# Polysketch attention and a multiplicative FFN on one core: six w3 blocks brought into w_out's column order by GpSimd's addition instead of by VectorE's transpose

## The chip, the cores and the metric

One Trainium2 chip, one of its cores. The metric is device time in microseconds of one execution of the whole program, as a median of several runs. Inputs of the reference that are float64 (S1, S2 and the four FFN matrices) lie in memory as 64-bit words, and the kernel turns them into float32 itself.

## The reference

```python
# batch 4, heads 4, seq 1088, head_dim 32, r = 8
def phi(x):
    a = np.einsum('rd,bhsd->bhsr', S1, x)
    b = np.einsum('rd,bhsd->bhsr', S2, x)
    return np.einsum('bhsi,bhsj->bhsij', a, b).reshape(*x.shape[:-1], r * r)
q_p, k_p = (phi(q), phi(k))
kv = np.einsum('bhsf,bhsd->bhfd', k_p, v)
z = np.sum(k_p, axis=2)
num = np.einsum('bhsf,bhfd->bhsd', q_p, kv)
den = np.einsum('bhsf,bhf->bhs', q_p, z)[..., None] + 1e-06
attn = (num / den).astype(np.float32)
# bridge: (B,H,S,D) -> (B*S, H*D); n_tokens 4352, d_model 128, d_ff 1024
a = x @ w1
b = x @ w2
h = a * b @ w3            # w3 is 1024 x 1024
out = (h @ w_out).astype(np.float32)
```

## The kernel before

The kernel is a list of named steps. Each step issues one or a few instructions on one engine, and the text ORDER at the head of the file says in which order all of them are issued. Each engine (TensorE for matmuls and transposes into PSUM, VectorE, ScalarE, GpSimd, and SyncE, which issues most DMAs) works through its own steps in that order, and waits at a step whose inputs or whose buffer are not ready. A second text, POOL, names the steps of a choosable kind that run on GpSimd; those not named there (or in ACTS) run on VectorE. A third, SLOTS, says which buffer each new tile takes: "x" (three buffers for k, v and q), "raw" (three, for raw weights), "l", "m", "s" and the eight PSUM banks "b". Nothing is scheduled at run time.

Names of the steps that matter below (b or g is a batch or group number):

- k{b}.load, .loadr, .max, .g, .lead, .rest, .gram0 to .gram4, .Gm, .Gt, .Ga, .Gb, .T, .N, .kT, .ab, .abt, .kp0, .kp1, .kv, .kq: the side of k. k is cut into a leading part and a rest (lead on ScalarE or VectorE, rest a subtraction), gram products give denominators' statistics, kp is the product of the two sketches, kv the product with v. kr0 and kr1 are the last 64 positions of two batches each; kr0.tr transposes them on TensorE.
- q{g}.tr, .max, .l2, .l1, .rm, .C0, .A0, .C1 (sketch products on TensorE), .Ct, .At (VectorE transposes), .sm, .st, .sh, .sl, .sc, .al, .p01, .p2, .p12, .dn, .de, .rc, .bs, .phi0 and .phi1 (the feature product), .pT0 and .pT1 (VectorE transpose), .x0 (TensorE, gives the attention output), .xT: the side of q. q0 and q1 have 512 positions, q2 and q3 too, q4 and q6 1024, qr the remainders.
- w{n}.load, .c, .m (ScalarE: upper words to float32 but for three bits of exponent, lower words scaled to an integer), .j (VectorE: a shift left by three), .a0 and .a1 (GpSimd: the integer addition of the lower part, in two halves of 512 columns): conversion of the weights. w0 and w1 hold halves of w1 and w2, w2 is w_out, w3 to w10 are the eight blocks of 128 rows of w3.
- f{ko}.t, .m, .o: the fold. The product of w3 and w_out is formed once (w3o = w3 @ w_out, eight blocks), since the FFN has nothing between the two. f.t transposes a w3 block (blocks 0 and 1 by TensorE in t0 and t1 with copies c0 and c1; blocks 2 to 7 by VectorE), f.m multiplies by w_out, f.o copies to SBUF. Both ways take the columns c, c+8, c+16, ... of w3, since w_out is loaded with 8 neighbouring rows in each partition.
- g{g}.{c}a, .c, .b, .m, .o: the FFN for group g (512 positions; gr has 256) and column block c: a and b are the matmuls with w1 and w2, c is ScalarE's copy of a, m is VectorE's product, o the matmul with w3o. g.oT and g.st bring the output out.
- warm*: matmuls on zeros that fill TensorE at the start.

The FFN's a and b matmuls of early groups are spread between the attention steps of later batches, so TensorE has work while VectorE prepares q and k.

Of the kernel before, what the change touches and what calls it, by code (L numbers as in the profile page):

```python
# [14 lines left out]
I32 = mybir.dt.int32  # L15
# [3 lines left out]
ALU = mybir.AluOpType  # L19
# [10 lines left out]
        "012345670123462764153276410574210437201420126754201640321407215350712047201326014235071352"  # L30
        "401547613720641602374651534672013635012731504705021746501456732142531602563623654321034562"
        "017567034617460315614370165425601351036450126305412036531024135605242556245645340467416701"
        "45701530507113274",
    "k_g": "0101",
    "l": "0123456789abc01243598a67b291a45c73b1a859076b2c9436071acb4326097a540cb261348",
    "m": 
        "0123456789abcdefghijklmnopqrstuv031425786badrenfoht514m3cjl6hqgsn58dmchr4qdj16u9krf2pi8b13"
        "ef750av9obrtlehnp4jfisbmugk07redgl5qrvocp6fre5ahldm2obl4thgq1pnreaq8g1npt7rglj925lujev62s4"
        "i9ajnrb1pe",
    "q_m": "0101101",  # L40
    "raw": "012012101201201",
    "s": "012345671302456703265140376215073",
    "x": "012010210210",
# [4 lines left out]
BY_PE = (0, 1)  # L48
# [4 lines left out]
    k0.Nf k0.Nh k0.Nl k0.kp0 k1.kp0 k2.kp1 k3.kp1 q0.p12 q0.p2 q0.phi0 q1.al q1.p12 q1.p2 q2.al q2.p12  # L53
    q2.phi0 q3.al q3.p2 q3.phi0 q4.al q6.al q6.p12 q6.p2 q6.phi0 qr.p12 qr.phi0 s.Pp s.blk s.blkh s.rest
    s.sum
# [18 lines left out]
v1.loadr q0.xT warm12 kr1.ab warm11 g0.2a g0.1a k2.load q1.pt0 q1.pt1 w1.j k1.Ga g0.3a g0.2c k1.kT1 q1.pc0 w1.a1
q1.pc1 k1.Gb k1.ab k1.T0 k1.T1 q1.x q3.tr g0.1c warm15 w0.a1 q1.restT q3.max g0.1b q2.tr k1.abt q1.xT k2.max g1.6b
g0.2b q2.max w1.a0 q2.l2 g1.3a s.AR k2.g k1.Ta k1.Tb g0.2m k2.lead0 k1.Ts q3.l2 g0.3c g1.3c q2.l1 k2.rest0 g0.7a g1.5a
g1.2a w2.load g1.5c w3.c k1.N0 q3.l1 g1.2c k1.N1 s.RC k1.kp1 q2.load g0.7c k1.Na g0.1m q4.tr k2.gram0 k2.gram1
k2.gram2 k2.gram3 k2.gram4 warm13 g1.0a kr1.abc g1.0c w3.m g1.6a g1.6c w4.load k2.Gm q4.max k1.Nb g0.0a g0.5a g0.5c
q2.rm g0.4b g1.2b q3.rm g0.0c k1.Nr w4.c k2.Gt g1.6m g0.7b q2.C0 k2.Ga w3.j g1.2m k2.Gb k3.zero w4.j k1.kp0 w4.m w3.a1
q2.A0 k3.loadr w4.a0 g0.7m q2.C1 q2.Ct q2.At q2.sm q2.st q2.sh q2.sl q2.sc q2.p01 k0.kqt w4.a1 g0.4a g0.6a g1.7a f1.t0  # L80
g0.6b g0.0b k0.kq w2.c g0.6c q4.l2 f1.c0 w3.a0 w2.j g0.0m g0.4c w2.m g1.5b g0.4m g1.1a g1.4a g1.1c g1.7c f0.t1 q2.al
v1.load w5.load f0.t0 w5.m k1.kv0 q2.p2 w2.a0 f0.c0 q2.p12 g0.6m k1.kv2 k1.kv3 q2.dn g1.5m k1.kv1 k2.T0 k2.T1 k1.kvr
k2.Ta q2.de q2.restT w9.load k1.kvc f0.c1 q2.rc k2.Tb k2.Ts q2.bs q3.C0 q3.A0 q3.C1 k1.kqt w2.a1 k1.kq w9.c f1.t1
q3.load g1.3b f0.m q3.Ct q3.At g1.7b k2.N0 q3.sm q2.phi0 f1.c1 f0.o q2.pT0 k2.N1 q2.x0 g1.4c q3.st g1.3m q3.sh w9.m
w5.c warm26 k2.Na q3.sl w8.load q3.sc f1.m g1.0b q2.xT0 k2.Nb w5.j k2.Nr v2.zero g1.7m q3.p01 q3.al g2.0a q4.l1 f1.o
g2.4b g2.0b q4.rm w9.j w5.a0 w6.load q4.C0 w9.a0 g2.0c w8.c q4.A0 w8.m q4.C1 w8.j g2.0m g2.4a g2.4c g1.0m q4.Ct q4.At
q3.restT w5.a1 g1.4b g2.2a g0.5b g2.3a g2.1a k3.load f2.t g2.2c w6.c w6.m g2.1c f2.m w9.a1 f6.t g1.1b f6.m k3.max w6.j
k3.g g0.5m q4.sm q3.p2 w8.a1 g2.3c kh2.load w7.load k2.kT0 g2.4m g2.1b g2.6a w6.a1 w6.a0 w8.a0 g2.5a g1.1m k3.lead0
g2.5c q3.p12 f5.t k3.rest0 g2.5b g2.3b f5.m g2.6c f5.o g2.7a f2.o w7.m f3.t q3.dn q3.de q3.rc f3.m q3.bs g2.6b q3.phi0
g2.1m g2.3m g2.5m g1.4m g2.2b q3.pT0 g2.7c f3.o w7.c k2.kT1 q3.x0 k3.gram0 k3.gram1 kr1.kp g2.2m q3.xT0 f6.o g2.6m  # L90
w7.j w7.a1 k3.gram2 k3.gram3 k2.ab k2.abt k3.gram4 k3.Gm g3.1a g3.5a g1.0o g3.6a g1.1o g1.6o g3.3a k3.Gt v3.zero
k2.kp1 qr.max k3.Ga v3.loadr w10.load g3.3c w7.a0 q4.st f4.t g3.1c g0.3b q4.sh q4.sl g3.6c qr.l2 w10.c g0.3m k2.kp0
q4.sc q4.p01 w10.j g3.5c k3.Gb w10.m g3.2b w10.a0 w10.a1 g3.4a g3.7a g2.7b qr.l1 v2.loadr v2.load kh3.load g3.4c g3.7c
q6.tr q6.max q6.l2 g0.0o g0.1o f4.m f4.o q6.l1 g0.2o g2.7m g0.6o g0.3o g0.5o g3.7b k2.kv0 q4.al k3.T0 q4.p2 q4.p12
q4.dn q4.de k3.T1 k2.kv3 f7.t q4.rc k3.kT0 k2.kv1 k2.kv2 k2.kvr warm28 g1.3o k2.kvc f7.m g3.2a q4.bs q4.phi0 f7.o
g3.2c q4.phi1 qr.rm k3.Ta v3.load g3.0a q4.pT0 k3.Tb g3.2m g0.4o g1.4o g0.7o k2.kqt k2.kq g1.5o g1.2o g3.0c g0.oT
q4.pT1 k3.Ts g3.7m k3.kT1 q4.x0 q4.x1 q4.xT1 q4.xT0 k3.N0 k3.N1 g1.7o k3.ab k3.Na k3.Nr k3.Nb q6.rm q6.C0 q6.A0 q6.C1
k3.abt g1.oT q6.Ct g2.0o g5.7a g3.3b g2.4o g4.0a g4.0c g5.7c q6.At q6.sm k3.kp0 k3.kp1 g2.6o g2.5o g4.1a g3.0b g3.0m
g3.3m k3.kv0 k3.kv1 q6.st k3.kv3 k3.kv2 k3.kvr qr.C0 qr.A0 k3.kvc qr.C1 k3.kqt g1.st g0.st qr.Ct qr.At g4.3a g2.3o
g5.0a q6.sh q6.sl q6.sc q6.p01 q6.al q6.p2 q6.p12 g5.4a qr.sm k3.kq g4.1c g4.4a g5.1b g5.1a g5.4c g5.1c g5.0c g4.7a  # L100
q6.dn qr.st g5.1m q6.de g4.3c qr.sh q6.rc g3.4b g2.2o g5.6a q6.bs g4.4c q6.phi0 g5.6c q6.phi1 g3.4m q6.pT0 g2.1o g2.7o
g4.0b q6.pT1 g5.0b g3.0o g4.7c g4.0m q6.x0 g2.oT q6.x1 g5.7b g5.2b q6.xT1 q6.xT0 qr.sl qr.sc g5.0m qr.al qr.p01 qr.p2
g3.6b g4.3b g3.6m qr.p12 g6.6a g6.0a g6.6b g6.0c g6.6c g5.2a g3.1b g6.6m g4.3m g6.4a g5.3a g5.5a g5.7m g5.2c g6.4c
g3.1m qr.dn qr.de g5.2m g7.1a g4.5a qr.rc qr.bs qr.phi0 g5.5c g5.3c g5.4b g5.4m g4.5c g3.5b g4.5b g7.1c g3.4o g6.4b
g7.7a g3.5m g6.1a g5.3b g2.st g4.5m g7.6a g6.1c g7.7c g4.4b g6.5a g5.5b g7.0a g6.4m qr.pT0 g5.3m g7.0c g3.3o g4.4m
g5.5m qr.x0 g3.1o g3.6o g3.2o g6.5c g7.6c qr.xT0 g3.5o g4.6a g4.7b g6.3a g5.0o g4.6c g7.5b g7.6b g7.6m g4.7m g6.1b
g6.2b g5.1o g6.5b g6.7a g6.3c g6.7c g6.5m g7.0b g5.2o g5.4o g5.6b gr.0a gr.0c g6.1m g5.6m g5.3o g7.0m g7.5a g5.5o
g6.2a g7.5c g7.0o g7.4a g6.2c g7.4c gr.6a gr.6c g3.7o g7.3a g7.4b g5.6o g6.0b g7.5m g7.4m g6.2m gr.4b gr.0b gr.0m
g7.3b g4.2a g7.3c g3.oT g4.2c gr.1a g5.7o g5.oT gr.1c gr.6b g4.1b gr.6m g7.3m g6.7b g6.7m g4.0o g4.1m g7.6o g4.4o
g4.1o g6.0m g7.2a g7.2c gr.4a gr.4c g7.1b g6.0o g7.5o g7.7b g7.1m g7.7m gr.4m g6.3b g6.5o g7.2b g7.2m gr.3b gr.3a  # L110
# [11 lines left out]
def make_steps(ctx, tc, q, k, v, S1, S2, moe_w1, moe_w2, moe_w3, moe_w_out, out):  # L122
# [3 lines left out]
    r = S1.shape[0]  # L126
    DM, DF = moe_w1.shape
    assert (B, H, S, D, r, DM, DF) == (4, 4, 1088, 32, 8, 128, 1024)
    NC = DF // 128
# [18 lines left out]
    def on(name):  # L148
        return pool if name in POOL else act if name in ACTS else dve
# [236 lines left out]
    def conv(n):  # L386
# [41 lines left out]
        @step(f"w{n}.j")  # L428
        def _():
            on(f"w{n}.j").tensor_scalar(made(), x["c"].bitcast(I32), 3, None, ALU.logical_shift_left)  # L430
# [1125 lines left out]
```

## Time and profile before

| | us |
|---|---|
| median of 3 runs | 255.98 (255.94 to 256.82) |
| profiled execution | 256.87 |
| its span, first to last instruction | 255.0 |
| TensorE matmuls busy | 247.4 |
| VectorE busy | 170.3 |
| ScalarE busy | 99.6 |
| GpSimd busy | 63.4 |

The granted clock of TensorE is 1.00 throughout. Of the rows of a group, the first figures after the bar are the busy time in us and the mean time of one instruction in ns, then the idle time just before them and what ended it. In a timeline a row has its start, its length in us, the engine, the source line, the operation, out<-in, the shape, and in brackets the idle time before it and its releaser.

### The profile page before, as it was taken

To read this page: it belongs to the slowest core of one execution; us is meant where nothing else is said; L and a number is where in the kernel's file an instruction comes from. 1 tells how busy PE (TensorE), PEld (TensorE's weight loads), DVE (VectorE), ACT (ScalarE), POOL (GpSimd) and SP (SyncE) were. 2 spreads that over 40 slices of the span, in tenths; PEclk is the share of its full clock that TensorE was granted. 3 is DMA by queue.
4 is the path that set the end of the run, shared out by engine and by line. 5 is a ranking of instruction groups with operands and counts; after the bars stand their busy time and mean duration, and the time that the engine had idled before them with its cause. 6 is when DMAs were issued, how large, how long until landed. Compare 5 with 4: busy or idle time off the path is not lost.

```text
span 255.0 us, 6027 instructions
## 1 busy us (share of the span) xinstructions
PE 247.4 (97%) x2519; PEld 139.8 (55%) x2519; DVE 170.3 (67%) x357; ACT 99.6 (39%) x185; POOL 63.4 (25%) x99
## 2 busy tenths in 40 slices
PE   8799999999999998999999999999999999999994
PEld 6689746456835575465544544444444445445454
DVE  3799999999999998998887667455202314432222
ACT  3668558886866541274131141241320132101000
POOL 2385560475364534422003044010000000000000
PEclk9999999999999999999999999999999999999999
DMA  6959383692897200990005000200000002200133
GB/s 181 282 160 269 125 322 141 177 234 69 226 219 200 48 3 3 195 228 2 3 3 82 5 0 1 41 1 3 0 0 0 3 0 36 46 0 0 29 54 63
DMA packets 30267, 22.02 MB, mean 86 GB/s; under 512 B 21152, under 2 KB 25504, under 8 KB 29856
## 3 DMA queue, kind: packets, MB, share of 16 engines
q1 hardware_dynamic: 29552, 21.05, 32.2%
q10 hardware_dynamic: 688, 0.59, 0.7%
q8 instruction: 20, 0.33, 0.5%
q14 instruction: 7, 0.06, 0.1%
HBM read 19.40 MB, written 2.23 MB: 85 GB/s over the span
## 4 chain that ended last, share of the span: by engine, by line
PE 74%; DVE 19%; DMA 2%; issue 2%; SPq 1%; POOL 1%; ACT 0%; DVEq 0%; POOLq 0%
PE ps_o L1462 22%; PE a_ps L1439 20%; PE b_ps L1449 19%; DVE ab L1455 3%; DVE w3T L463 2%; PE ps_g L595 2%; PE ps_x L1399 2%; DMA kr<-in_k_dram 2%; PE ps_or L1469 1%; PE ps_w3o L469 1%; PE ps_kv L705 1%; PE ps_ac L1285 1%; DVE kk L587 1%; DVE k_m L180 1%; DVE pT L1388 1%
## 5 line engine op out<-in xcount | busy, mean ns | idle before, releaser
L1455 DVE TENSOR_TENSOR ab<-ffa,b_ps 128x512 f32<-128x512 f32 (+1 forms) x72 | 45.3, 650 | 53.7 <-PE b_ps L1449 45.5
L1444 ACT COPY ffa<-a_ps 128x512 f32<-128x512 f32 (+1 forms) x72 | 38.4, 564 | 103.3 <-PE a_ps L1439 97.7
L1439 PE MATMUL a_ps<-xT,w 128*128 128x512 f32 (+1 forms) x144 | 66.0, 572 | 0.0
L1449 PE MATMUL b_ps<-xT,w 128*128 128x512 f32 (+1 forms) x144 | 65.9, 570 | 0.0
L1462 PE MATMUL ps_o<-ab,w3o 128*128 128x512 f32 x128 | 61.3, 595 | 0.0
L1439 PEld LDWEIGHTS a_ps<-xT,w 128*128 128x128 f32 x144 | 26.6, 191 | 29.1 <-issue 23.4
L1449 PEld LDWEIGHTS b_ps<-xT,w 128*128 128x128 f32 x144 | 26.6, 191 | 27.5 <-issue 23.4
L1462 PEld LDWEIGHTS ps_o<-ab,w3o 128*128 128x128 f32 x128 | 23.8, 191 | 24.7 <-issue 24.3
L436 POOL TENSOR_TENSOR w3c<-w3c,cv_m 128x512 int32<-128x512 int32 x16 | 20.6, 1306 | 22.4 <-DVE w3c L430 10.1
L469 PEld LDWEIGHTS ps_w3o<-wo,w3T 128*128 128x128 f32 x128 | 15.3, 192 | 4.5 <-issue 2.1
L469 PE MATMUL ps_w3o<-wo,w3T 128*128 128x128 f32 x128 | 15.7, 276 | 0.5 <-DVE w3T L463 0.5
L221 PE MATMUL idle_ps<-zeros 128*128 128x256 bf16 x72 | 13.4, 317 | 1.0 <-DVE zeros L193 1.0
L1478 DVE STREAM_TRANSPOSE oT<-ps_o 128x512 f32<-128x512 f32 x8 | 5.7, 708 | 12.0 <-PE ps_o L1462 12.0
L229 ACT ACTIVATE cv_c<-raw 128x1024 f32<-128x1024 f32 x11 | 12.9, 1172 | 1.3 <-DMA raw<-in_moe_w_dram 1.3
L1380 POOL TENSOR_TENSOR ph<-s_al,s_bs 128x1024 f32<-128x1024 f32 (+1 forms) x4 | 8.0, 1991 | 20.2 <-DVE s_bs L1370 20.2
L417 ACT ACTIVATE cv_m<-raw 128x1024 int32<-128x1024 uint32 x11 | 13.0, 1189 | 0.0
L463 DVE STREAM_TRANSPOSE w3T<-w3c 128x1024 f32<-128x1024 f32 x6 | 12.1, 2034 | 0.0
L613 POOL TENSOR_TENSOR kp<-kabt 128x1024 f32<-128x1024 f32 x3 | 5.8, 1946 | 18.5 <-DVE kabt L681 18.2
L221 PEld LDWEIGHTS <-zeros 128*128 128x128 bf16 x72 | 7.7, 114 | 4.0 <-issue 1.2
L1388 DVE STREAM_TRANSPOSE pT<-ph 128x1024 f32<-128x1024 f32 (+1 forms) x7 | 8.0, 1151 | 1.7 <-POOL ph L1380 1.7
L1410 ACT COPY xT<-ps_x 128x128 f32<-128x128 f32 (+2 forms) x20 | 4.6, 326 | 10.0 <-PE ps_x L1399 7.0
L180 DVE TENSOR_REDUCE k_m<-k 128x1 f32<-128x1152 f32 (+1 forms) x5 | 5.4, 1086 | 3.1 <-DMA k<-in_k_dram 3.1
(243 smaller groups left out, 296.6 us busy)
## 6 DMA issues: line engine op xcount, KB each, us to landing
raw<-in_moe_w_dram SPq DMA_DIRECT2D x24, 256.0 KB, 5.9
qh<-in_q_dram SPq DMA_DIRECT2D x4, 544.0 KB, 4.2
out_dram<-oT SPq DMA_DIRECT2D x33, 64.0 KB, 2.0
raw<-in_moe_w_dram SPq DMA_DIRECT2D x4, 512.0 KB, 6.0
raw<-in_moe_w_dram SPq DMA_DIRECT2D x2, 1024.0 KB, 8.1
k<-in_k_dram SPq DMA_DIRECT2D x3, 512.0 KB, 5.2
v<-in_v_dram SPq DMA_DIRECT2D x2, 512.0 KB, 4.0
raw<-in_moe_w_out_dram SPq DMA_DIRECT2D x1, 1024.0 KB, 5.8
```

The costliest lines, as they stand in the source:

```text
L221: pe.matmul(t, zeros, bview(zeros, [[0, 2], [1, 128]]), start=True, stop=True)
L229: act.activation(dst, hi.bitcast(F32), ACT.Prelu, scale=2.0 ** -112, alpha=-2.0 ** 32)
L417: act.mul(x["m"], words(0).bitcast(U32), 2.0 ** -29)
L436: pool.tensor_tensor(d, d, x["m"][:, i * 512:(i + 1) * 512], ALU.add)
L463: dve.transpose(w3T[ko].rearrange("p s (i r) -> p s i r", r=32), bview(w3c[ko], [[1, NC], [256, 4], [NC, 32]]))
L469: pe.matmul(t["o"], w3T[ko][:, c], wo[:, c], start=c == 0, stop=c == NC - 1)
L1388: dve.transpose(s["pT"][:, cut], s["ph"][:, cut])
L1439: pe.matmul(x["a"][:, :w], w_of(0, c), xT[g][:, c0:c0 + w], start=True, stop=True)
L1444: act.copy(x["s"][:, :w], x["a"][:, :w])
L1449: pe.matmul(x["b"][:, :w], w_of(1, c), xT[g][:, c0:c0 + w], start=True, stop=True)
L1455: dve.tensor_mul(ab_sb[g, c][:, c0:c0 + w], x["s"][:, :w], x["b"][:, :w])
L1462: pe.matmul(o_ps[g], w3o[:, c], ab_sb[g, c], start=c == 0, stop=c == NC - 1)
```

## The change

In w5 to w10 (w3's blocks 2 to 7) the shift w.j now works in place in cv_c, and GpSimd's addition writes its sum to a new w3c tile in another order of columns: column 8a + b of each 256 goes to place 32b + a. Its two inputs are read in order, and each next word is written 32 words (128 bytes) further, in runs of eight. The VectorE transpose f.t then reads 32 neighbouring columns where it read every eighth. Blocks 0 and 1, and the other weights, are converted as before and as whole blocks; blocks 0 and 1 are still transposed by TensorE.

```diff
         @step(f"w{n}.j")
         def _():
-            on(f"w{n}.j").tensor_scalar(made(), x["c"].bitcast(I32), 3, None, ALU.logical_shift_left)
+            d = x["c"].bitcast(I32) if 3 <= n and n - 3 not in BY_PE else made()
+            on(f"w{n}.j").tensor_scalar(d, x["c"].bitcast(I32), 3, None, ALU.logical_shift_left)
 
         for i in range(2):
             @step(f"w{n}.a{i}")
             def _(i=i):
+                if 3 <= n and n - 3 not in BY_PE:
+                    if i == 0:
+                        made()
+                    d, c, m = (y[:, i * 512:(i + 1) * 512].rearrange(f"p (j {o}) -> p j a b", j=2, **z) for y, o, z in (
+                        (x["d"].bitcast(I32), "b a", {"a": 32}), (x["c"].bitcast(I32), "a b", {"a": 32}),
+                        (x["m"], "a b", {"a": 32})))
+                    pool.tensor_tensor(d, c, m, ALU.add)
+                    return
                 d = x["d"].bitcast(I32)[:, i * 512:(i + 1) * 512]
                 pool.tensor_tensor(d, d, x["m"][:, i * 512:(i + 1) * 512], ALU.add)
...
-                dve.transpose(w3T[ko].rearrange("p s (i r) -> p s i r", r=32), bview(w3c[ko], [[1, NC], [256, 4], [NC, 32]]))
+                dve.transpose(w3T[ko].rearrange("p s (i r) -> p s i r", r=32), bview(w3c[ko], [[32, NC], [256, 4], [1, 32]]))
```

With it POOL, SLOTS and ORDER are new as a whole. On GpSimd and no longer on VectorE are k1.kp1, k2.rest0, k3.kp0, q0.phi1, q2.p2, q3.p12, q4.phi1, qr.p2 and s.low; the other way went q0.phi0, q2.al, q3.phi0, q6.p12, q6.p2, qr.p12, s.blkh and s.rest. The number of instructions on each engine is the same.

In ORDER, at the front, kr0.tr leaves its place ahead of k0.gram0 and comes behind k0.N1:

```diff
-k0.max1 k0.g k0.tr1 k0.lead0 warm5 c.act k0.tr0 s.words k0.lead1 s.pair k0.rest0 k0.rest1 s.low kr0.load kr0.tr
-k0.gram0 k0.gram1 k0.gram2 s.lead k0.gram3 s.sum s.rest k0.gram4 s.T s.four s.tc s.P s.R k0.kT0 q0.tr warm1 k0.Gm
...
+warm18 s.four s.lead warm8 warm12 k0.rest1 s.low s.sum k0.gram0 k0.gram1 k0.gram2 k0.gram3 q0.tr k0.gram4 s.rest s.T
...
+s.Pp k1.max q0.C0 k0.N0 k0.N1 k0.abc0 warm25 k0.kp0 v0.loadr kr0.tr q0.sma k0.kT1 k0.Na k0.ab1 q0.sta q1.l2 w0.m k0.Nb
```

In SLOTS, "x" gives k1 the buffer of k0 (it had one of its own, and v0 had k0's):

```diff
-    "x": "012010210210",
+    "x": "012020120201",
```

SyncE's loads at the front are now k0.loadr, s, q0, w0, k1, k1.loadr, kr0, v0.loadr, v0, w1 (before: k0.loadr, s, q0, kr0, k1, k1.loadr, w0, v0, q1, v0.loadr), and v3.load comes behind g1.st.

On VectorE the steps between q2's and q3's transposes are now: q2.pT0, k2.Ts, q3.st, q3.sh, q3.sl, q3.sc, k2.Na, g1.0m, g0.3m, k2.Nb, w8.j, q3.p01, k2.Nr, q4.rm, g1.3m, w5.j, g2.2m, w6.j, q4.At, q4.Ct, g0.0m, g1.1m, f2.t, k3.max, f3.t, q3.dn, k3.g, g1.4m, g1.7m, q3.de, w9.j, f5.t, g2.1m, g2.0m, f6.t, q4.sm, q3.rc, q3.bs, k2.kT0, q4.st, q3.phi0, q3.pT0, and behind it w7.j and k3.rest0. Beside them on GpSimd: q2.phi0, w6.a0, w5.a0, q3.al, w5.a1, q3.p2, w6.a1, w8.a0, w8.a1, q3.p12, w9.a0, w9.a1, w7.a0, w7.a1. Before, the four transposes f2, f6, f5 and f3 stood in the same stretch, with their additions (w5, w9, w8, w6) mostly ahead of it.

At w1 and w2, GpSimd's steps are now w0.a0, w1.a0, k2.rest0, w1.a1, s.RC, w0.a1, and the matmul g1.6b stands ahead of w1.a1 in ORDER, so that this one block of w2 enters g1 with its upper words alone.

## The prediction

> **What bounds the kernel now.** I read the page's engine totals and groups first, then busy time by stages, then TensorE's timeline at its idle places, then the operations that the change touches. The totals and three groups:
>
> ```profile
> span 255.0 us, 6027 instructions
> ...
> PE 247.4 (97%) x2519; PEld 139.8 (55%) x2519; DVE 170.3 (67%) x357; ACT 99.6 (39%) x185; POOL 63.4 (25%) x99
> ...
> PE 74%; DVE 19%; DMA 2%; issue 2%; SPq 1%; POOL 1%; ACT 0%; DVEq 0%; POOLq 0%
> ...
> L436 POOL TENSOR_TENSOR w3c<-w3c,cv_m 128x512 int32<-128x512 int32 x16 | 20.6, 1306 | 22.4 <-DVE w3c L430 10.1
> ...
> L463 DVE STREAM_TRANSPOSE w3T<-w3c 128x1024 f32<-128x1024 f32 x6 | 12.1, 2034 | 0.0
> ...
> L1388 DVE STREAM_TRANSPOSE pT<-ph 128x1024 f32<-128x1024 f32 (+1 forms) x7 | 8.0, 1151 | 1.7 <-POOL ph L1380 1.7
> ```
>
> TensorE is busy for 97% of the span, so VectorE's time counts only where TensorE waits for it. The chain says where: all of its long VectorE part lies ahead of 97 us. Busy time by stages (length, PE, PEld, DVE, ACT, POOL):
>
> ```profile
> 30.00:66.40 36.40, 36.40 (x526) 20.37 (x524) 34.36 (x88) 26.09 (x43) 17.51 (x20) 1.00 0.63 190
> 66.40:97.10 30.70, 29.39 (x273) 17.29 (x271) 30.46 (x51) 18.34 (x28) 13.73 (x12) 1.00 0.52 125
> 97.10:130.00 32.90, 32.85 (x414) 18.44 (x423) 29.49 (x46) 11.38 (x23) 7.83 (x7) 1.00 0.37 83
> 130.00:255.00 125.00, 121.70 (x736) 60.09 (x712) 52.10 (x104) 24.38 (x55) 8.93 (x7) 1.00 0.11 19
> ```
>
> From q2's transpose (ends 66.4) to q3's (ends 97.0) VectorE rests 0.24 us in 30.7. After 97 us TensorE hardly rests until the tail. Its real waits, in its timeline:
>
> ```profile
> 8.34 0.30 PE L755 MATMUL ps_krt<-ident,kr 128*128 128x128 f32 x1 [1.43 <-DMA kr<-in_k_dram]
> ...
> 89.38 2.02 PE L469 MATMUL ps_w3o<-wo,w3T 128*128 128x128 f32 x16 [0.21 <-DVE w3T L463]
> ...
> 92.57 2.02 PE L469 MATMUL ps_w3o<-wo,w3T 128*128 128x128 f32 x16 [0.31 <-DVE w3T L463]
> ...
> 97.15 1.07 PE L1399 MATMUL ps_x<-pT,kq 32*32 32x128 f32 x64 [0.83 <-DVE pT L1388]
> ```
>
> These are 1.43 us at the front and 1.35 us at the end of VectorE's full stretch: 2.8 us. The order is written out by hand for every engine, so what TensorE multiplies later is the same work; whatever it gains by q3.x0 (the 97.15 row) it keeps to the end, if nothing new waits behind.
>
> **The change, part by part.** The method: I add the instructions of each engine in the new order, each with its time to the next start in the old trace, and lay on it the waits that the new order names.
>
> Transposes: six at 2034 become six like L1388's 128x1024 rows (mean 1226 by form): 6 x 0.81 = 4.9 us less on VectorE. Four (f2, f3, f5, f6) lie in the full stretch: 3.2 us. VectorE's queue from the end of q2.pT0 to the end of q3.pT0 sums to 30.4 us in the old order (measured 30.65) and 27.2 in the new; the other steps that enter and leave cancel.
>
> Engine swaps: GpSimd takes k1.kp1 and k3.kp0 (1.95 each by L613's row on it), k2.rest0 (not shown there; 1152 elements at L613's 1.90 or L1380's 2.24 ns each, 2.2 to 2.6, I take 2.2, the plainer pattern), q4.phi1 (1.95 to 2.99) and small ones, and gives q0.phi0, q3.phi0, q6.p2, q6.p12 and others back: net some 5 us more. k2.rest0 ends near 36.2, its gram is reached near 38.4: hidden by 2 us; without that cover its 2.2 would show. w1.a1 stands behind it on GpSimd, but g1.6b has been put ahead of w1.a1 and waits for nothing.
>
> The addition itself now writes words 128 bytes apart; inputs stay in order. No row shows GpSimd writing so. Below nothing I exclude more than 0.2 us (L436 takes 2.55 ns an element, the quickest product of 512 on GpSimd 1.07 us, 2.09 ns). Above, the nearest strided row is VectorE's old transpose, 2034 for 1226: 66%, or 0.84 us more for each half. I take nothing: that strided stream ran at 1.99 ns an element, quicker than GpSimd's 2.55 with words in line, so a write stream of its own has time to spare; patterns in runs of eight (L1380) cost GpSimd nothing extra either. I keep -0.2 to +0.84. [...]
>
> The new wait in the stretch: count from the end of q2.pT0. VectorE ends w6.j at 8.9 and comes to f2.t at 12.1. GpSimd has four things between (w6.a0, w5.a0, q3.al, w5.a1: 3 x 1.27 + 0.46), so f2.t starts at 13.2: 1.1 us of waiting. Queued behind it on VectorE are k3.max, f3.t and q3.dn; q3.dn waits for q3.p12, behind q3.p2, w6.a1, w8.a0 and w8.a1 on GpSimd: done at 17.9, 1.2 us of waiting. w9.j ends at 20.3, its two halves at 22.9: 0.2 us at f6.t. Sum 2.5. So 27.2 + 2.5 = 29.7; q4.st stood in the old trace beside w7.a0 on GpSimd and took 1.72 us for an instruction that is else 0.65, so 28.7 to 29.7 against 30.65: 0.9 to 2.0 won, middle 1.5.
>
> The front: kr0.tr moves behind k0.N1, so k0.gram0 no longer stands behind the 1.43 us; the gram ends near 9.5 (rest1 ends 8.43, then 0.36 + 0.36 + 0.24) and not 10.4. VectorE's 1.34 us of idleness before k0.Gm is filled by s.rest and q1.tr. Its queue up to q2.pT0 is 55.9 us for 58.2. Of these 3.6 us the walk gives back 1.9 (k1.Na behind the N matmuls, k2.Gm behind its gram, q2.Ct behind TensorE), so q2.pT0 ends 1.7 earlier, at 64.7. k1's load now reuses k0's buffer and waits for k0.gram4: issued near 9.6, not 4.16, with kr0 and v0 queued behind it on SyncE. At 4.0 to 5.2 us from issue to landing (512 KB rows) k1 lands at 13.6 to 14.8 for a k1.max at 14.0, v0 at 16.7 to 17.9 for a k0.kv0 at 17.6: hidden, barely. v3.load is put behind g1's output on SyncE, lands near 135, and is wanted at 142.
>
> The sum: q3.pT0 ends at 97.0 - 1.7 - 1.5, about 93.9 (94.4 at worst). TensorE's own queue to q3.x0 is 84.8 us (85.0 before). Its idleness by then was 12.15; less 1.43 and 1.35, plus 0.7 for two new waits (g0.7a behind ScalarE's w3.m and w3.c, q3.C0 behind g0.5m), it is 10.1: q3.x0 at 95.0 for 97.15. TensorE's queue, not VectorE, is then last by about 1 us. Next late would be k3.rest0, now behind q3.pT0 (ends 95.8, gram reached 95.7): even. f4.t and f7.t end 1 to 2 us ahead of their matmuls. So 2.2 us, carried to the end. The profiled execution took 256.87 with its span of 255.0, 0.89 above the median; I put the difference on the median: 255.98 - 2.2 = 253.8.
>
> **The rivals.**
>
> GpSimd's strided write is slow. It decides in the stretch, where eight halves (w6, w5, w8, w9) stand in VectorE's way: q3.x0 is the later of 95.0 and 93.9 + 8p. The gain is gone at p = 0.41 us, the time is over 0.5% longer from p = 0.57. At 0.84, q3.x0 comes at 100.6, 3.4 us late: 259.4. For it: the only strided row of the trace pays 66%. Against: GpSimd's slower pace. [...]
>
> The front gain does not come: k1, kr0 or v0 lands over 1.5 us later than I reckon, since SyncE issues them one behind the other after 9.6. Then q3.pT0 ends near 95.6 and TensorE comes near 96.4: 0.75 won, 255.2. For it: the DMA queue carried 217 GB/s in the first 10 us, and w0's 1 MB stands ahead.
>
> Later matmuls wait: the second half's order is wholly new, and output steps g*.o come some 20 us earlier in places; PSUM banks then wait for VectorE. At 2 to 4 us of it, 256 to 258. Against: VectorE is busy 52 of 125 us after 130.
>
> **How the numbers follow.** About 0.5% (1.28 us) is what a measurement of this kernel can tell from no change. Forecast 0.52 (252.3 to 254.7); front gain lost 0.20 (within 0.5%); slow strided write 0.18, with its part over p = 0.57; later waits 0.10, slower. So faster 0.52, same 0.20, slower 0.28. If all waits shown and half a microsecond of small bubbles went, 3.4 to 3.7 us would be won: the low end 252.3. The high end is the slow write, 259.4.
>
> **What would show it.** L463's line (moved down nine) at about 1230, L436's line still near 1300; f2.t and q3.dn idle on VectorE for about 1.1 us each, on GpSimd; no DMA wait before k0.gram0; q3.x0 near 95.0 with no wait for pT, and TensorE dense behind it. Wrong, if additions take over 1.7 us, if VectorE idles by the front loads, or if TensorE shows waits after 100 us.

## The result, and the profile after

The changed kernel is slower: 259.92 us (median of 4 runs, 259.76 to 260.24) beside 256.38 for the kernel before on the same chip; the ratio is 1.0139 (95% interval 1.0124 to 1.0154). The prediction said 253.8, with a range from 252.3 to 259.4. Of all the runs in this document one, 261.96 us in e10 at a granted clock of 0.98, counts as slow and is out of the ratios and ranges given. The page of the profiled execution (260.24 us), its totals, its chain and three groups:

```profile
span 258.5 us, 6026 instructions
...
PE 249.7 (97%) x2519; PEld 140.7 (54%) x2519; DVE 165.9 (64%) x357; ACT 98.7 (38%) x185; POOL 71.6 (28%) x99
...
PE 89%; DVE 8%; issue 1%; ACT 0%; POOL 0%; DVEq 0%
...
L442 POOL TENSOR_TENSOR w3c<-cv_c,cv_m 128x512 int32<-128x512 int32 x12 | 16.8, 1424 | 19.3 <-DVE cv_c L431 19.3
...
L1397 DVE STREAM_TRANSPOSE pT<-ph 128x1024 f32<-128x1024 f32 (+1 forms) x7 | 8.0, 1157 | 3.9 <-POOL ph L1389 3.8
...
L472 DVE STREAM_TRANSPOSE w3T<-w3c 128x1024 f32<-128x1024 f32 x6 | 7.3, 1225 | 1.1 <-POOL w3c L442 1.1
```

The six transposes fell from 12.1 us to 7.3, VectorE as a whole by 4.4, and yet the span grew by 3.5. Busy time by stages, cut again at the ends of q2's and q3's transposes (length, PE, PEld, DVE, ACT, POOL):

```profile
30.00:70.60 40.60, 39.18 (x585) 22.22 (x572) 34.83 (x95) 28.64 (x46) 25.00 (x24) 1.00 0.70 191
70.60:99.10 28.50, 28.50 (x272) 17.50 (x270) 25.69 (x49) 17.24 (x28) 11.23 (x11) 1.00 0.65 161
99.10:130.00 30.90, 30.28 (x386) 17.16 (x386) 27.57 (x47) 8.18 (x17) 12.61 (x9) 1.00 0.07 20
130.00:258.50 128.50, 125.17 (x751) 61.05 (x749) 53.22 (x106) 26.43 (x61) 8.44 (x6) 1.00 0.13 23
```

The full stretch is shorter, as forecast: 28.5 us for 30.65. The loss lies ahead of it and behind it. q2.pT0 starts at 69.31 where it started at 65.20 (4.1 us late); the stretch wins 2.1 of that back; q3.x0 starts at 99.35 for 97.15 (2.2 late), and behind it 1.3 us more are lost.

Ahead of q2.pT0, single instructions of VectorE take several times what they took before. The first one is k0.Ts, an addition of 32x32 elements. VectorE's timeline and, below it, GpSimd's at the same place, in the changed kernel:

```profile
14.06 0.67 DVE L954 SCALAR_TENSOR_TENSOR q<-q,qT 128x512 f32<-128x512 bf16 x1
14.65 1.93 DVE L850 TENSOR_TENSOR T_p<-T_p 32x32 f32<-32x32 f32 x1
16.52 1.33 DVE L180 TENSOR_REDUCE k_m<-k 128x1 f32<-128x1152 f32 x1
```

```profile
14.12 2.43 POOL L622 TENSOR_TENSOR kp<-kab 128x1024 f32<-128x1024 f32 x1
```

and the same two instructions in the kernel before:

```profile
14.86 0.17 DVE L841 TENSOR_TENSOR T_p<-T_p 32x32 f32<-32x32 f32 x1
```

```profile
14.87 1.98 POOL L613 TENSOR_TENSOR kp<-kab 128x1024 f32<-128x1024 f32 x1 [0.61 <-ACT kab L644]
```

Before, k0.Ts began 0.01 us ahead of GpSimd's k0.kp0 and took 0.17. Now k0.kp0 is released 0.75 us earlier, k0.Ts begins behind it, and ends 0.04 us after it. The same happens at the last instruction of k1.Ta (1.04 for 0.18 us, beside k2.rest0, which is new on GpSimd), k1.Nr (1.24 for 0.17, beside w3.a0), q0.phi0 (1.57 for 0.69, beside q0.phi1, the two having changed engines), k1.g, q1.sh, q0.de, q1.de and q3.rm (0.3 to 0.4 each). Over what their like take alone, that is 6.1 us of VectorE up to q2.pT0; in the kernel before I find 2.4 to 2.6 (q2.sh 1.0, q1.de 0.4 and smaller ones).

What these instructions have in common is two inputs in SBUF. In the whole trace of the changed kernel, 12 such VectorE instructions began while a product or sum of GpSimd had a quarter of a microsecond or more still to run: all 12 ended after it, and took 0.43 to 1.93 us. Some 60 with one input in SBUF or none began in the same way, and none of them took over 0.05 us more than the median of its like. How the one holds up the other is not shown.

My theory was then: the edit is sound, and the new order lost the time by such stalls ahead of q2.pT0. The rivals: the strided addition costs after all; or the loads that were moved at the front (k1, kr0, v0) make it late.

### The profile page after: what moved, and what is told of

It is laid out like the page before. It is cut to its first block, busy times and chain, and to the rows that moved or that the text cites. A ratio compares the mean times of both kernels' runs of the same rounds, so it can differ in the third digit from the quotient of the medians.

```text
span 258.5 us, 6026 instructions
## 1 busy us (share of the span) xinstructions
PE 249.7 (97%) x2519; PEld 140.7 (54%) x2519; DVE 165.9 (64%) x357; ACT 98.7 (38%) x185; POOL 71.6 (28%) x99
## 4 chain that ended last, share of the span: by engine, by line
PE 89%; DVE 8%; issue 1%; ACT 0%; POOL 0%; DVEq 0%
PE b_ps L1458 23%; PE a_ps L1448 22%; PE ps_o L1471 21%; PE ps_w3o L478 6%; PE idle_ps L221 3%; PE ps_x L1408 2%; PE ps_g L604 2%; PE ps_ac L1294 2%; PE ps_or L1478 1%; PE ps_kv L714 1%; PE ps_ab L672 1%; PE ps_wt L463 1%; DVE ph L1135 1%; DVE k_m L180 1%; PE ps_kt L630 0%
## 5 line engine op out<-in xcount | busy, mean ns | idle before, releaser
L1471 PE MATMUL ps_o<-ab,w3o 128*128 128x512 f32 x128 | 60.5, 594 | 0.0
L442 POOL TENSOR_TENSOR w3c<-cv_c,cv_m 128x512 int32<-128x512 int32 x12 | 16.8, 1424 | 19.3 <-DVE cv_c L431 19.3
L1389 POOL TENSOR_TENSOR ph<-s_al,s_bs 128x1024 f32<-128x1024 f32 (+1 forms) x4 | 6.9, 1734 | 41.4 <-DVE s_bs L1379 41.4
L622 POOL TENSOR_TENSOR kp<-kabt 128x1024 f32<-128x1024 f32 x5 | 9.7, 1951 | 15.3 <-DVE kabt L690 14.5
L221 PE MATMUL idle_ps<-zeros 128*128 128x256 bf16 x72 | 12.4, 318 | 1.0 <-DVE zeros L193 1.0
L604 PE MATMUL ps_g<-kk 128*32 128x64 f32 x288 | 7.7, 224 | 1.1 <-ACT xT L1419 0.6
L472 DVE STREAM_TRANSPOSE w3T<-w3c 128x1024 f32<-128x1024 f32 x6 | 7.3, 1225 | 1.1 <-POOL w3c L442 1.1
## 6 DMA issues: line engine op xcount, KB each, us to landing
raw<-in_moe_w_dram SPq DMA_DIRECT2D x24, 256.0 KB, 5.7
```

The costliest lines, as they stand in the source:

```text
L221: pe.matmul(t, zeros, bview(zeros, [[0, 2], [1, 128]]), start=True, stop=True)
L442: pool.tensor_tensor(d, c, m, ALU.add)
L604: pe.matmul(o[h * D:(h + 1) * D], lhs, rhs, start=start, stop=stop, skip_group_check=True)
L622: eng.tensor_mul(dst, bview(av, [list(av.ap[1]), list(av.ap[2]), [0, r]]), bview(bv, [list(bv.ap[1]), [0, r], list(bv.ap[2])]))
L1471: pe.matmul(o_ps[g], w3o[:, c], ab_sb[g, c], start=c == 0, stop=c == NC - 1)
```

## The experiments

**e1, the edit alone.** Order and engines of before; the addition and the transposes as in the change's diff, with the new tile still taken at w.j, and the slots "l" dealt anew.

```diff
-            on(f"w{n}.j").tensor_scalar(made(), x["c"].bitcast(I32), 3, None, ALU.logical_shift_left)
+            d = made()
+            if 3 <= n and n - 3 not in BY_PE:
+                d = x["c"].bitcast(I32)
+            on(f"w{n}.j").tensor_scalar(d, x["c"].bitcast(I32), 3, None, ALU.logical_shift_left)
```

> The order and the engines of the kernel before; only the six additions write in w_out's column order and the six transposes read neighbouring columns (the shift goes in place, and the slots of the tiles that it keeps longer are dealt anew). Theory (the edit itself is sound, the new order lost the time by instructions of VectorE that have both inputs in SBUF and start beside a GpSimd instruction): additions 1.27 us, transposes 1.23, VectorE's queue from q2.pT0 to q3.pT0 up to 3.2 us shorter, q3.x0 no longer behind VectorE, so at 95.6 to 96.2 instead of 97.15: 254.4 to 255.2 us. Rival (the strided write or the cheaper transposes cost elsewhere): 256 or more.

**e2, the order alone.** The changed kernel with additions in line and transposes as before.

```diff
-                    d, c, m = (y[:, i * 512:(i + 1) * 512].rearrange(f"p (j {o}) -> p j a b", j=2, **z) for y, o, z in (
-                        (x["d"].bitcast(I32), "b a", {"a": 32}), (x["c"].bitcast(I32), "a b", {"a": 32}),
-                        (x["m"], "a b", {"a": 32})))
+                    d, c, m = (y[:, i * 512:(i + 1) * 512] for y in (x["d"].bitcast(I32), x["c"].bitcast(I32), x["m"]))
...
-                dve.transpose(w3T[ko].rearrange("p s (i r) -> p s i r", r=32), bview(w3c[ko], [[32, NC], [256, 4], [1, 32]]))
+                dve.transpose(w3T[ko].rearrange("p s (i r) -> p s i r", r=32), bview(w3c[ko], [[1, NC], [256, 4], [NC, 32]]))
```

> The changed kernel's order, engines and slots, with the additions writing in line and the six transposes reading every eighth column as before. Theory: transposes 2.03 us, four of them in the full stretch, so q3.x0 comes up to 3.2 us later than in the changed kernel (99.35): 261.5 to 263.2 us. Rival (the loss comes from the strided additions): 256 to 258 us.

e1 gave 254.45 us beside 256.57 (ratio 0.9915, 0.9888 to 0.9942), e2 262.43 (1.0226, 1.0198 to 1.0253). Both fall in the theory's figures and outside the rival's. The edit wins 2.1 us in the old order and 2.5 in the new one (262.43 to 259.92); the new order loses about 6 with the edit out. Totals and groups of e1, and then the two groups of e2:

```profile
span 252.6 us, 6022 instructions
...
PE 246.9 (98%) x2519; PEld 139.8 (55%) x2519; DVE 164.5 (65%) x357; ACT 99.7 (39%) x185; POOL 64.1 (25%) x99
...
L442 POOL TENSOR_TENSOR w3c<-cv_c,cv_m 128x512 int32<-128x512 int32 x12 | 16.0, 1353 | 17.7 <-ACT cv_m L417 8.1
...
L472 DVE STREAM_TRANSPOSE w3T<-w3c 128x1024 f32<-128x1024 f32 x6 | 7.3, 1226 | 1.2 <-POOL w3c L442 1.2
```

```profile
L440 POOL TENSOR_TENSOR w3c<-cv_c,cv_m 128x512 int32<-128x512 int32 x12 | 16.8, 1428 | 21.1 <-DVE cv_c L431 21.0
...
L470 DVE STREAM_TRANSPOSE w3T<-w3c 128x1024 f32<-128x1024 f32 x6 | 12.2, 2034 | 0.7 <-POOL w3c L440 0.7
```

In one and the same order the addition takes 1424 ns with the strided write and 1428 without: the write in steps of 128 bytes adds nothing that these means show. The tile view of w3c in the changed kernel (minimum, median, maximum in ns) shows why the mean is over 1.3 us: a few of the twelve are held up, and the median isn't:

```profile
L442 POOL TENSOR_TENSOR w3c<-cv_c,cv_m x12: 1273/1284/2271, 79.2 to 114.1; 128x512 int32<-128x512 int32 x12
L445 POOL TENSOR_TENSOR w3c<-w3c,cv_m x4: 1264/1278/1643, 48.4 to 64.3; 128x512 int32<-128x512 int32 x4
```

**e3, k0.Ts with one input in SBUF.**

```diff
+            if b == 0:
+                dve.tensor_copy(a["Tp"][:, 2], a["T"][:, 0])
+                dve.tensor_add(a["Tp"][:, 2], a["Tp"][:, 2], a["T"][:, 1])
+                return
             dve.tensor_add(a["Tp"][:, 2], a["Tp"][:, 0], a["Tp"][:, 1])
```

> The changed kernel, but k0.Ts takes its two terms from PSUM (a copy of one, then an addition with one SBUF input) and not two SBUF inputs. Theory: its 1.93 us were spent waiting for k0.kp0 on GpSimd, which began 0.5 us earlier; with one SBUF input it doesn't wait, both instructions take 0.35 us together, k1.max starts at 14.9 to 15.1 instead of 16.52, and up to 1.5 us of it reaches the end: 258.4 to 259.9 us. Rival (the front is late because k1, kr0 or v0 land late): k1.max starts no earlier, time 259.9.

259.45 us (ratio 1.0107, 1.0075 to 1.0140), 0.5 better than the changed kernel, in intervals that overlap, so that the evidence is the trace. VectorE's timeline:

```profile
14.46 0.17 DVE L851 COPY T_p<-ps_T 32x32 f32<-32x32 f32 x1
14.66 0.17 DVE L852 TENSOR_TENSOR T_p<-T_p,ps_T 32x32 f32<-32x32 f32 x1
14.77 1.35 DVE L180 TENSOR_REDUCE k_m<-k 128x1 f32<-128x1152 f32 x1
...
18.70 1.23 DVE L622 TENSOR_TENSOR kp<-kab 128x1024 f32<-128x1024 f32 x1 [1.17 <-ACT kab L653]
```

k0.kp0 ran on GpSimd from 13.92 to 16.35, and neither instruction waited for it: 0.35 us for 1.93, k1.max at 14.77. But a good 1.2 of the 1.75 us were given back at once, at k0.kp1, and TensorE's timeline has the reason:

```profile
17.05 0.30 PE L764 MATMUL ps_krt<-ident,kr 128*128 128x128 f32 x1 [1.08 <-DMA kr<-in_k_dram]
```

kr0, issued by SyncE behind k1 at 11.5 and 12.2, lands at 16.92. So the rival on the loads is true as well, one step behind the stall: while k0.Ts waited for GpSimd, it hid the late load.

**e4, the stall put into the kernel before.** Here and below, lines of ORDER are cut to the steps around those that move.

```diff
-k0.Tb q0.l2 q0.l1 q0.rm warm17 k0.Ts k0.ab0 q1.l2 k0.abc0 w0.load warm7 warm4 k0.ab1 s.Pp s.blkh s.zero q0.restT q0.A0
+k0.Tb q0.l2 q0.l1 q0.rm warm17 k0.ab0 q1.l2 k0.abc0 w0.load warm7 warm4 k0.ab1 s.Pp s.blkh s.zero q0.restT k0.Ts q0.A0
```

> The kernel before with one instruction of VectorE moved one place back: k0.Ts behind q0.restT, so that it starts 0.2 us later, when k0.kp0 has begun on GpSimd (in the kernel before it starts 0.01 us ahead of it). Theory: k0.Ts takes about 1.7 us instead of 0.17 and ends with k0.kp0, k1.max starts at 16.6 to 16.9 instead of 15.13; what of it reaches the end is between 0 and 1.6 us, since VectorE rests for 0.5 us before k1.Ga and again behind k1.Ts: 256.0 to 257.6. Rival (a swap of two steps for whose results nothing waits is free): k0.Ts 0.17, time 256.0.

258.12 us (1.0052, 1.0021 to 1.0082): one small instruction, one place later, and the kernel before is 1.2 to 1.5 us slower. VectorE's and GpSimd's timelines:

```profile
14.33 0.23 DVE L904 STREAM_TRANSPOSE qT_rest<-qh 128x64 f32<-128x64 f32 x1
14.49 1.84 DVE L841 TENSOR_TENSOR T_p<-T_p 32x32 f32<-32x32 f32 x1
16.26 1.33 DVE L180 TENSOR_REDUCE k_m<-k 128x1 f32<-128x1152 f32 x1
```

```profile
14.34 1.95 POOL L613 TENSOR_TENSOR kp<-kab 128x1024 f32<-128x1024 f32 x1 [0.61 <-ACT kab L644]
```

q2.pT0, q3.x0 and the last matmul are each 1.2 us later than in the kernel before. The loss lies within the 0 to 1.6 us that were forecast, near its upper end: little of the stall was given back. The time lies above 257.6 because the kernel before took 256.57 beside this run and not the 256.0 that the forecast started from.

**e5, the load of kr0 early, on top of e3.**

```diff
-k0.g k0.lead0 s.pair k0.lead1 warm22 q0.load warm5 k0.tr0
+k0.g k0.lead0 s.pair k0.lead1 warm22 q0.load kr0.load warm5 k0.tr0
...
-k0.T1 s.blkh s.Pm s.zero s.Pc k0.Ta k0.Tb q1.max q0.l1 warm16 warm13 k0.ab0 warm27 warm1 kr0.load q0.A0 q0.rm k0.Ts
+q0.l2 k0.T0 k0.T1 s.blkh s.Pm s.zero s.Pc k0.Ta k0.Tb q1.max q0.l1 warm16 warm13 k0.ab0 warm27 warm1 q0.A0 q0.rm k0.Ts
```

> The kernel of e3 (k0.Ts from PSUM), and kr0.load moved ahead of w0.load on SyncE, where the kernel before has it. In e3 k0.Ts was free, but TensorE then waited 1.08 us for kr0 (landed 16.92) at kr0.tr, and k0.kp1 started at 18.70 instead of 19.18. Theory (two causes, one behind the other): the wait for kr0 goes, k0.kp1 starts at 17.4 to 17.8; what later instructions lose beside GpSimd (q0.phi0 0.9, k1.g 0.4, k1.Ta 0.9, k1.Nr 1.1 us) stays; 258.3 to 259.3 us. Rival (late landings are the whole of it): over 2 us better than e3, under 257.5.

258.50 us (1.0108, 1.0064 to 1.0151); the runs were 258.2 to 258.8, and the profiled one 261.15. The wait for kr0 is gone (kr0.tr at 15.36), but in the profiled execution k1, whose load waits for k0's buffer, landed at 17.22 and not at 14.2 to 14.8 as in the changed kernel, e3 and e6. What held it up is not shown: e6 and e9 issue the same loads in the same order, and there it landed at 14.19 and 13.87.

```profile
17.34 1.35 DVE L180 TENSOR_REDUCE k_m<-k 128x1 f32<-128x1152 f32 x1 [2.95 <-DMA k<-in_k_dram]
```

So the median fits the theory. k0.kp1's start can't be read from this execution; in e9, which keeps both edits, it is 17.04. The prediction's "hidden, barely" holds for k1 in the other profiled executions and not in this one.

**e7, k1.Nr alone moved** (the changed kernel).

```diff
-k2.gram1 k2.gram2 g1.6m k1.ab k2.gram3 k1.Na w1.a1
+k2.gram1 k2.gram2 g1.6m k1.ab k2.gram3 k1.Na k1.Nr w1.a1
```

> The changed kernel with one instruction moved: k1.Nr (0.14 us alone, 1.24 beside w3.a0) goes up behind k1.Na, where GpSimd and VectorE both rest. Theory: it takes 0.15 us there, VectorE is 1.1 us earlier from k1.abt on, and what of it isn't taken by the rest before q2.Ct (0.3 us) reaches q2.pT0: 68.5 or earlier for 69.31; time 259.2 to 259.7. Rival (its 1.24 us are its own): no change, 259.9.

259.29 us (1.0113, 1.0093 to 1.0132), 0.6 better than the changed kernel, within the theory's figures, though the two intervals overlap. In the changed kernel VectorE's k1.Nr and, below it, GpSimd's w3.a0 are

```profile
48.89 1.24 DVE L888 TENSOR_TENSOR AR<-RC,mask2n 128x16 bf16<-128x16 f32 x1
```

```profile
48.45 1.64 POOL L445 TENSOR_TENSOR w3c<-w3c,cv_m 128x512 int32<-128x512 int32 x1 [1.19 <-DVE w3c L431]
```

and in e7 k1.Nr is

```profile
45.20 0.18 DVE L888 TENSOR_TENSOR AR<-RC,mask2n 128x16 bf16<-128x16 f32 x1
```

q2.pT0 starts at 68.55, 0.76 earlier, and q3.x0 (98.61) and the last matmul are 0.74 and 0.75 earlier: what VectorE has won at q2.pT0 reaches the end whole.

**e6 and e9, the front freed.** e6 takes e5 and moves three stalled instructions; e9 is e6 with one more move.

In POOL q0.phi0 stands again, and q0.phi1 and k2.rest0 are out.

```diff
-s.KS k2.lead0 g1.6a g1.3a k2.rest0 q2.load s.AR q2.tr
+s.KS k2.lead0 g1.6a g1.3a q2.load s.AR q2.tr
...
-q2.max k1.Ta k1.Tb q3.tr k1.Ts q2.l2
+q2.max k1.Ta k1.Tb q3.tr k1.Ts k2.rest0 q2.l2
...
-k2.gram1 k2.gram2 g1.6m k1.ab k2.gram3 k1.Na w1.a1
+k2.gram1 k2.gram2 g1.6m k1.ab k2.gram3 k1.Na k1.Nr w1.a1
```

> The kernel of e5, and three instructions put where no GpSimd product or addition runs beside them: q0.phi0 back on GpSimd and q0.phi1 on VectorE, k2.rest0 back on VectorE behind k1.Ts (where VectorE rested for 2.1 us), k1.Nr moved up behind k1.Na. Theory: q0.phi on VectorE 0.71, k1.Ta 0.52, k1.Nr 0.15 us; with k0.Ts and kr0 some 4 us of VectorE's delay are gone, q2.pT0 starts at 65 to 66.5 instead of 69.31, q3.x0 at 96 to 97.5, the time is 256.0 to 257.5 us. Rival (VectorE's stalls are given back in its rests, TensorE's order sets the time): no better than 259.

e6 was slower, 261.31 us (1.0186, 1.0164 to 1.0208). It was a poor edit of mine: q0.phi1 went to VectorE but kept its late place in the order, so it ran at 25.47, and TensorE waited for it. TensorE's row, and then its busy time by single microseconds with the granted clock (the column behind the five engines):

```profile
26.49 0.90 PE L1157 MATMUL ps_ph<-ident,ph 128*128 128x128 f32 x3 [2.70 <-DVE ph L1137]
```

```profile
24.50:25.50 1.00, 0.00 (x0) 0.00 (x0) 0.90 (x5) 0.00 (x0) 0.53 (x2) 1.00 0.96 351
25.50:26.50 1.00, 0.01 (x1) 0.01 (x1) 1.00 (x3) 0.00 (x0) 0.39 (x1) 0.64 0.86 290
26.50:27.50 1.00, 1.00 (x5) 1.00 (x6) 1.00 (x3) 0.00 (x0) 0.59 (x1) 0.50 0.04 14
...
31.50:32.50 1.00, 1.00 (x65) 1.00 (x58) 0.14 (x1) 0.00 (x0) 0.00 (x0) 0.50 0.06 16
32.50:33.50 1.00, 1.00 (x78) 0.96 (x69) 0.00 (x0) 0.00 (x0) 0.00 (x0) 0.94 0.00 0
```

About 2 us into this rest of 2.70 us the clock fell to half (0.50), and it stayed there for some 6.8 us, so that k1's gram (30.84 to 33.5) was late too. A rest of 2.49 us in e5, which ended at 19.95, left the clock at 1.00; what decides between the two is not shown.

So e9 moves q0.phi1 up as well:

```diff
-q1.st k1.kT1 q0.pt0 q0.scy k1.rest0
+q1.st k1.kT1 q0.pt0 q0.scy q0.phi1 k1.rest0
...
-k0.kz q1.scy q0.phi1 k2.zero
+k0.kz q1.scy k2.zero
```

> The kernel of e6 with q0.phi1 moved up on VectorE behind q0.scy. In e6 it had stayed where the changed order has it for GpSimd, so on VectorE it ran at 25.47, TensorE rested 2.70 us for it at q0.pt1, and behind that rest the granted clock was 0.58 to 0.74 for 10 us. Theory: without that rest the three freed instructions and k0.Ts show: q0.pt1 waits less than 0.5 us, k1.gram0 at 25.6 to 27, q2.pT0 at 64.5 to 66.5 (69.31 in the changed kernel, 65.20 before), q3.x0 at 95.5 to 97, 255.3 to 256.8 us. Rival (the new order has further waits of its own of the same size): q2.pT0 over 67, time over 257.3.

e9: 256.97 us (1.0018, 1.0005 to 1.0030), 2.95 better than the changed kernel and 0.2 above the theory's upper end. q0.phi1 takes 0.68, the last instruction of k1.Ta 0.18, k1.Nr 0.18; q0.pt1 waits no more and k1.gram0 starts at 25.96; q2.pT0 starts at 65.56 for 69.31, q3.x0 at 95.59 for 99.35, and the last matmul is 3.76 earlier. That is more than the 2.95 of the medians, and 0.6 of it came ahead of all the moved instructions: k0's gram ended at 9.69 in this execution and at 10.29 in the changed kernel's. The rival's figures (q2.pT0 over 67, over 257.3 us) did not come, but the new order has smaller waits of its own, which are shown below.

**e10, k1 with a buffer of its own, on top of e9.** 
```diff
-k0.g k0.lead0 s.pair k0.lead1 warm22 q0.load kr0.load warm5
+k0.g k0.lead0 s.pair k0.lead1 warm22 q0.load k1.zero kr0.load k1.load k1.loadr warm5
...
-k0.Gb q0.max k0.kT0 k1.zero k1.load k1.loadr s.blk
+k0.Gb q0.max k0.kT0 v0.zero s.blk
...
-    "x": "012020120201",
+    "x": "012002102021",
```

> The kernel of e9, and k1 gets a buffer of its own again (v0 takes k0's), so that k1's load is issued near 4 us behind kr0 and not at 9.7 behind k0.gram4. Theory: k1 landed at 14.2 in e6 for a k1.max at 14.36, so it is hidden in most executions and this gives within 0.3 us of e9, with less spread (in e5 one execution of four was 2.6 us longer, with k1.max waiting 2.95 us for k1). Rival (loads still bound the front of e9): over 0.7 us better than e9.

257.13 us (1.0025, 1.0011 to 1.0039): within 0.3 of e9, so the loads don't bound e9's front. The smaller spread that I expected did not show (256.4 to 257.4 there, 256.6 to 258.0 here).

**e11, k3.rest0 early** (the changed kernel). 
```diff
-q3.bs k2.kT0 q4.st f5.m f6.m q3.phi0 q3.pT0 g1.1o w7.j g2.7c k3.lead0 k3.rest0 g2.6c
+q3.bs k2.kT0 f5.m f6.m q3.phi0 q3.pT0 g1.1o g2.7c k3.lead0 k3.rest0 w7.j q4.st g2.6c
```

> The changed kernel with q4.st and w7.j moved behind k3.rest0 on VectorE. There k3.rest0 ends at 100.89 and k3.gram0 starts at 101.04, 0.85 us after TensorE is through with q3.x0: the step that I had called even. Theory: q3.pT0 ends 0.65 and k3.rest0 1.3 us earlier, k3.gram0 follows q3.x0 without a wait, and 0.5 to 0.9 us reach the end: 259.0 to 259.4 us. Rival (TensorE's later order makes up for it): 259.9.

260.00 us (1.0139, 1.0118 to 1.0160): the rival's figure, but not for its reason. k3.gram0 starts at 100.26 for 101.04 and waits no more, but 3 us later TensorE stands here,

```profile
103.17 0.64 PE L672 MATMUL ps_ab<-kT,KS 64*32 64x256 f32 x8 [0.46 <-DVE kT L665]
```

and q4.pT0 starts at 127.94 for 128.03. The wait is for k2.kT1, which VectorE starts at 102.42 for 102.51, since the queue ahead of it holds the same steps in another order. Just ahead of k2.kT1 q4.sh, with two inputs in SBUF, took 1.60 us beside w7's additions on GpSimd (1.78 in the changed kernel); no run moved that one.

**e8, kr0.tr out of the gram's way, on top of e1** (the PSUM slots of the steps between follow).

```diff
-s.words k0.lead1 s.pair k0.rest0 k0.rest1 s.low kr0.load kr0.tr
-k0.gram0 k0.gram1 k0.gram2 s.lead k0.gram3 s.sum s.rest k0.gram4 s.T s.four s.tc s.P s.R k0.kT0
+s.words k0.lead1 s.pair k0.rest0 k0.rest1 s.low kr0.load
+k0.gram0 k0.gram1 k0.gram2 s.lead k0.gram3 s.sum s.rest k0.gram4 s.T s.four s.tc s.P s.R kr0.tr k0.kT0
```

> The kernel of e1 (the edit alone in the order of before), and kr0.tr moved behind s.R on TensorE, so that the gram no longer stands behind the load of kr0 (1.43 us). It tests the front's term by itself. As I reckoned it in the prediction: the gram ends at 9.5 to 9.7 instead of 10.46, k0.Gm starts at 9.6 to 9.9 instead of 10.52, q2.pT0 is up to 0.9 us earlier, 253.4 to 254.2 us. Rival (VectorE or another wait is next there): the gram is earlier, but k0.Gb or k0.Ts is not, and the time stays at 254.4; if k0.kp0 on GpSimd comes to start ahead of k0.Ts, 255 to 256.

254.08 us (0.9912, 0.9897 to 0.9926): the best of all, 0.9% under the kernel before. In TensorE's timeline the gram now starts with k0.rest0 and no longer behind kr0:

```profile
7.60 0.33 PE L604 MATMUL ps_g<-kk 128*32 128x64 f32 x7 [1.20 <-DVE kk L596]
```

It ends at 9.62 and k0.Gm starts at 9.68, as reckoned; q2.pT0 is 0.86 earlier than in the kernel before, but only 0.29 earlier than in e1, whose profiled execution waited 0.81 us for kr0 and not 1.43. From e1 the gain is 0.4 us, within what the two intervals leave open.

## Why the prediction was wrong

**Right: the transposes, the addition, the stretch.** 1225 ns for 1226. The addition's extra p, for which I had kept -0.2 to +0.84, is 0.00 (e2 beside the changed kernel), so the slow strided write is out as a rival. The waits that I had read out of the order came where I put them: VectorE waits 0.72 us at f2.t, 0.92 at q3.dn and 0.41 at f6.t, 2.05 in all for 2.5. The stretch took 28.5 us, a little under the 28.7 to 29.7 that I had said.

**Right: what VectorE wins at q2.pT0 or q3.pT0 is kept to the end.** e4 (1.17 us late there, 1.16 at the end), e7 (0.76, 0.75) and e9 (3.75, 3.76) show it from both sides. In e3 part was lost: 0.85 us at q2.pT0, 0.64 at q3.x0, 0.49 at the end.

**Wrong: the front.** The step that failed is the sum of VectorE's queue up to q2.pT0 (55.9 us for 58.2, and q2.pT0 to end at 64.7; it ended at 70.56). I added each instruction's duration in the old trace as if it were its own. For instructions with two SBUF inputs it is not: it depends on what GpSimd runs at that moment (k0.Ts took 0.17 us in the kernel before and 1.93 in the changed one), and with 5 us more put on GpSimd and every start moved, other pairs meet. Counted in the same way (to the start of q2.pT0, without rests of over 0.1 us), the queue was 58.2 us before and 59.3 in the changed kernel. Some 3.6 of the 5.9 us by which q2.pT0 ended too late are such stalls, by the rows (6.1, less the 2.5 that the old durations held already); e9, which takes away four of them and the late kr0, gets back 3.75, of which 0.6 is the gram's. I had the row for it and used it for one term only: I noted that q4.st took 1.72 us beside w7.a0 for "an instruction that is else 0.65", and left it at that.

**Wrong in size: the waits of the new order.** VectorE's rests of over 0.1 us up to q2.pT0 were 3.2 us before; less the 1.34 that was to be filled and with the 1.9 that the walk gives back, 3.8 were forecast. They were 5.9 in the changed kernel and 5.3 in e9. The walk had its 1.9 us at k1.Na, k2.Gm and q2.Ct. There, and at g1.6m just ahead of k1.Na, the rows have 4.1 us (3.4 in e9), and these are the two long ones, at g1.6m and k2.Gm:

```profile
44.08 0.69 DVE L1464 TENSOR_TENSOR ab<-ffa,b_ps 128x512 f32<-128x512 f32 x1 [2.15 <-ACT ffa L1453]
...
46.97 0.19 DVE L180 TENSOR_REDUCE G_g<-ps_g 128x1 f32<-128x32 f32 x1 [1.67 <-PE ps_g L604]
```

This is about the rest of the 5.9 us. No run took these waits away.

**The gram: late by TensorE's pace and not by the order.** It was to end at 9.5 and ended at 10.29. kr0.tr had gone, and twelve matmuls on zeros had come between k0.tr0 and k0.gram0. They are not the reason: with the same twelve the gram ended at 9.59 in e2 (the same order throughout) and at 9.64 to 9.69 in e5, e6 and e9, and without them at 9.62 in e8. What differs between these and the late ones (10.06 to 10.29 in the changed kernel, e3, e7 and e11) is TensorE's pace in the first microseconds. k0.tr0 in the changed kernel and in e2:

```profile
5.67 1.04 PE L630 MATMUL ps_kt<-ident,k 128*128 128x128 f32 x4
```

```profile
5.06 0.60 PE L628 MATMUL ps_kt<-ident,k 128*128 128x128 f32 x4
```

Until about 6.5 us in the changed kernel's profiled execution, and until about 4.4 us in e2's, a matmul on zeros starts every 0.21 us, and every 0.11 us after that. The profile gives the granted clock as 1.00 there too, and what sets the moment is not shown.

**The rival "the front gain does not come" had the place and not the cause.** It blamed the loads: kr0's would have cost 1.08 us (e3) and in one execution k1's 2.95 (e5), but in the changed kernel the stall of k0.Ts covers kr0's, and k1 landed at 14.79, ahead of k1.max at 16.52.

**Later waits.** "k3.rest0 even" cost 0.62 us of TensorE's time ahead of k3.gram0, and the second half as a whole 1.3. e9 loses the same 1.3 behind q3.x0, e1 in the old order nothing. e11 shows that the wait at k3.gram0 alone doesn't hold it; which of the later steps would have to move was not settled. Of the front, q2.pT0 in e9 is still 2.1 us behind my walk (63.45), 1.5 of them in the rests.

## What to carry to other kernels

Before you add up queues in a new order, mark the VectorE instructions that read two SBUF inputs and look which GpSimd work will run when each starts: here a 0.17 us addition took 1.93 (k0.Ts). When you give an engine swap a price, price the neighbours on both engines, and put such instructions into GpSimd's rests (k1.Nr: 0.18 us for 1.24 in e7), or take one input from PSUM (k0.Ts: 0.35 us for 1.93 in e3). Then add up the waits of the new order at every engine's hand-over, and look at more than one trace of the first microseconds. Judge an edit and the schedule that came with it apart: here the edit won 0.8% and the schedule lost over 2%.

## What the runs showed of the hardware that I had not expected

- GpSimd's 128x512 int32 addition writing words 128 bytes apart: median 1284 ns, in line 1278.
- GpSimd's instructions grew longer too: kr0.kp took 1.59 us beside VectorE's k0.kp1 (0.62 alone), q0.p2 1.44 beside k1.rest0 (0.50 in the kernel before).
- In the kernel before, two shifts with a single SBUF input (w2.j and w5.j) took 0.94 and 0.97 us for 0.69: both began while GpSimd ran q2.al and q3.al (0.69 and 0.46 us), and ended after them.
- In a rest of TensorE of 2.70 us its granted clock fell from 1.00 to 0.50, and stayed there for about 6.8 us (e6); a rest of 2.49 us (e5) left it at 1.00.
